# First batch, column 3: ordinary products for all score groups, and the sums of v made one column later

## The chip, the cores and the metric

The kernel runs on one core of one Trainium2 chip. The metric is the device time of one execution in microseconds (us): less is better. The times below are those of six executions, and one further execution was recorded by the hardware profiler. The engines are named as in the profile: PE (TensorE; PEld is its weight load), DVE (VectorE), ACT (ScalarE), POOL (GpSimd) and SP (SyncE). The last two issue most of the transfers here.

## The reference

There are 8 batches of 3008 rows. With S = 3008:

```
scores = (1/S) * z @ z.T                 # per batch, z: 3008 x 64
out    = (relu(scores) ** 2) @ v         # v: 3008 x 256
x      = u * out                         # u: 3008 x 256
h      = x @ w_in                        # 256 -> 2048
y      = (h * cos(h)) @ w_out            # 2048 -> 256
```

The square of the scores is symmetric, because the scores are z times its own transpose.

## The kernel before

**Tiling.** The 3008 rows of a batch are cut into 6 column blocks of 512 (the last has 448). A score group (b, c, R) is the 512x512 piece of the squared scores of batch b between column block c and row block R. It lives in one of 18 SBUF slots, `s0` to `s17`; the trace numbers them from s_70. For each column c the kernel sums, over all six row blocks R, the product of v with the group. The sum stands in two PSUM banks, `acc`, one for each half of the 256 columns of v. `finish` (line 377) multiplies it by u into `x`, and `h_quantum` and `y_quantum` (lines 515, 532) do the two matmuls after that, on tiles of 512 rows.

**Where a group comes from.** By symmetry a group with R > c, once computed, serves column R too, if it is transposed: `turn_s` (line 317) issues a DMA transpose on SP from the slot of the group to a second slot, the turned group. In the first batch the columns 0 to 2 don't wait for that: `direct` (line 234) says that all six of their groups are computed. From column 3 on the groups with R < c come turned. For column 3 of the first batch these are (0,0,3), (0,1,3) and (0,2,3). The list `TURNS` says when the transposes of the first three columns are issued.

**Two ways to multiply.** `av_bank` (line 359) is the ordinary one: for each block of 128 rows and each half of v, one matmul of 512 columns. Four blocks and two halves make 8 of them for one group. `product` (line 459) is the other: a 2x2 scheme with 7 instead of 8 products, of which each takes 2 matmuls of 256 columns for a group, 14 in all. It needs sums: of the group (`a_sums1` and `a_sums2`, lines 440 and 447, on DVE, in place and in an extra slot called "x"), of v (`v_sums`, line 405, three DVE instructions for one row block, kept for the whole batch), and of partial results (`keep`, line 491: three ACT copies and three DVE additions in a column). `seven` (line 254) lists the row blocks of a column that take this way: `WSET`, and none where `direct` holds. So in the first batch column 3 is the first column to use it, for R = 0, 1 and 2.

**Order.** All pieces are put in a list of events with a time and a rank (`at`, line 555), sorted, and issued in that order. The times are in steps, 8 steps to a column; a step comes to about 3 us of the chip. Within each engine that is the order of the instructions, apart from small moves by the layer that records them[...]. Matmuls are chained in one order (`chain`, line 109), and each load that POOL issues is held until the matmul that was issued last before it (`hold`, line 116). Scores are computed in visits (`s_visit`, line 324): up to three halves of groups, each with two matmuls into PSUM (line 270), two relus on ACT (line 306) and one squaring on DVE into the slot (line 308). Six PSUM banks, called `w`, serve scores, h and y alike, and there are three buffers `rt` for the relus and three `c` for the cosines.

**Slots.** `place` (line 590) goes through all lives of groups, turned groups and "x" slots by their first step, and gives each the slot that has been free the longest. A slot whose last reader is a transpose that has not yet landed makes its next writer wait on the chip, whatever the planner thought. At column 3 of the first batch the planner has:

- slot s_80: the group (0,1,3), read by its transpose; next, the "x" slot of column 3
- slot s_84: the group (0,1,4), read by its transpose; next, the group (0,3,4)
- the turned groups (0,0,3), (0,1,3), (0,2,3) in s_75, s_82, s_70

SP's queue has, in this order: (0,0,3), (0,0,4), a transpose of u, (0,0,5), (0,1,3), (0,1,4), (0,1,5), (0,2,3), (0,2,4), (0,2,5), (0,3,4), (0,3,5), and a transpose of u for column 3.

Of the kernel before, what the change touches and what calls it, by code (L numbers as in the profile page):

```python
# [14 lines left out]
def kernel(  # L15
# [25 lines left out]
    NC = NJ // K  # L41
# [5 lines left out]
    U = 8  # L47
# [25 lines left out]
    TSUM = [-2.9, -0.9, -0.8, 3.5, 3.5]  # L73
    XEND = 4.0
    WSET = {0: [0, 1, 2], 1: [0, 1, 2], 2: [0, 1, 2], 3: [0, 1, 2], 4: [0, 1, 2, 3], 5: [0, 1, 2, 3]}
# [28 lines left out]
    def after(ins, other, cls):  # L104
        tc.add_manual_dep(
            ins, other.name,
            mybir.DependencyInfo(cls, mybir.DependencyReason.DATA), reason="order")
# [126 lines left out]
    def direct(b, c, R):  # L234


        return b == 0 and c <= 2
# [15 lines left out]

    def seven(b, c):

        return [] if direct(b, c, c) else WSET[c]

    def s_matmuls(b, c, R, p):

# [75 lines left out]
    def av_half(b, c):  # L335

        a = fresh[(b, c, NC - 1)][K - 1]
        for nh in range(NDH):
            h = slice(nh * JLAST, (nh + 1) * JLAST)
            chain(nc.tensor.matmul(  # L340
                accs[(b, c)][nh],
                vs(b, NG - 1)[h, G - 1, nh * P:(nh + 1) * P],
                a[h], start=False, stop=False, skip_group_check=True))
# [25 lines left out]
    def av_chunk(b, c, blocks, start, last):  # L369
        if start:  # L370
            open_acc(b, c)
        for nh in range(NDH):
            av_bank(b, c, nh, blocks, start, last)
        if last:
            finish(b, c)
# [29 lines left out]
    def v_sums(b, R):  # L405

        j = R * K
        t = vs(b, j // G)[:, j % G:j % G + K, :].rearrange("p (h k) d -> p h k d", h=2)
        o = vsum[R]
        b12, b22 = t[:, :, :, P:2 * P], t[:, 1, :, P:2 * P]  # L410
        left = t[:, 0, :, :].rearrange("p k (d w) -> p d k w", w=P)
        after(nc.vector.tensor_tensor(o[:, 0:3:2], b12, left, ALU.subtract).ins,
              before[-1], NOSYNC)
        nc.vector.tensor_tensor(o[:, 1], b22, o[:, 0], ALU.subtract)
        nc.vector.tensor_tensor(o[:, 3], t[:, 1, :, 0:P], o[:, 1], ALU.subtract)
# [24 lines left out]
    def a_sums1(b, c, R):  # L440
        s1 = quarters(b, c, R, (0, 1))
        after(nc.vector.tensor_tensor(s1, s1, quarters(b, c, R, (1, 1)), ALU.add).ins,
              before[-1], NOSYNC)
        nc.vector.tensor_tensor(  # L444
            second(b, c, R), s1, quarters(b, c, R, (0, 0)), ALU.subtract)

    def a_sums2(b, c, R):

        src = quarters(b, c, R, (1, 0), (0, 1))
        dst = (quarters(b, c, R, (0, 1), (1, -1)) if by_key(b, c, R)  # L450
               else quarters(b, c, R, (1, 0), (-1, 1)))
        h = wide(b, c) // 2
        sub = second(b, c, R).unsqueeze(1).broadcast_to([P, 2, 2, h])
        after(nc.vector.tensor_tensor(dst, src, sub, ALU.subtract).ins,  # L454
              before[-1], NOSYNC)
# [35 lines left out]
    def keep(b, c, n):  # L491
        h = wide(b, c) // 2
        if n == 1:
            parts_of[(b, c)] = (spool.tile([P, 2, CW // 2], FP32, name="p15"),
                                spool.tile([P, 2, CW // 2], FP32, name="q"))
        p15, q = parts_of[(b, c)]
        acc = accs[(b, c)]
        if n in (1, 5):
            nc.scalar.copy(p15[:, n // 5, 0:h], acc[n // 5][:, h:2 * h])
        elif n == 6:  # L500
            nc.vector.tensor_tensor(  # L501
                q[:, 0, 0:h], acc[0][:, h:2 * h], p15[:, 1, 0:h], ALU.add)
        elif n == 8:
            nc.vector.tensor_tensor(
                acc[0][:, 0:h], acc[0][:, 0:h], p15[:, 0, 0:h], ALU.add)
        elif n == 7:
            nc.scalar.copy(q[:, 1, 0:h], acc[0][:, h:2 * h])
        else:
            a = acc[1][:, 0:2 * h].rearrange("p (t h) -> p t h", t=2)
            nc.vector.tensor_tensor(a, a, q[:, :, 0:h], ALU.add)  # L510
# [44 lines left out]
    def at(t, rank, f):  # L555
        events.append((t, rank, len(events), f))
# [5 lines left out]
    span = NC * U  # L562
# [5 lines left out]
    for b in range(B):  # L568
# [6 lines left out]
        for c in range(NC):  # L575
            if direct(b, c, c):
                for i in range(NC):
                    R = (c + i) % NC
# [7 lines left out]
    def use(key, first, last):  # L586
        a, z = lives.get(key, (first, last))
        lives[key] = (min(a, first), max(z, last))
# [16 lines left out]
                use(("a", b, c, R), t, t + 3)  # L605
    for b in range(B):
        for R in range(NW):
            at(b * span + (TSUM[R] if b else 2 * U + R), 2, lambda b=b, R=R: v_sums(b, R))
        for c in range(NC):
            t = b * span + c * U  # L610
            W = seven(b, c)
            d = direct(b, c, c)
            ready = 1.5 + when[(b, c, NC - 1)]
            first, last = (0.6, 6.93) if d else (HALF[c] if W else 1.0, 7.3)
            room = [i for i, sc in enumerate(scores)
                    if max(ready, t + first) < sc[0] < t + last and i not in also]
            if room:
                also[min(room, key=lambda i: scores[i][0])] = lambda b=b, c=c: av_half(b, c)
            else:
                at(t + last, 3, lambda b=b, c=c: av_half(b, c))  # L620
            if d:
                order = [(c + i) % NC for i in range(NC)]
            else:
                order = [R for R in range(NC) if R not in W]
            blocks = [R * K + k for R in order for k in range(K) if R * K + k < NJ - 1]
            if d:
                places = [(t + q + (0.5 if q < U - 1 else -0.05), 3) for q in range(U)]
            elif W:
                for i, R in enumerate(W):
                    at(t + SUM1[c][0] + SUM1[c][1] * i, 2, lambda b=b, c=c, R=R: a_sums1(b, c, R))  # L630
                    use(("x", b, c), t + SUM1[c][0], t + XEND)
                    use(("t", b, R, c) if R < c else ("a", b, c, R), t, t + 6.5)
                    at(t + SUM2[c][0] + SUM2[c][1] * i, 2.5, lambda b=b, c=c, R=R: a_sums2(b, c, R))
                at(t + WADD[c], 2.6, lambda b=b, c=c: keep(b, c, 0))
                at(t + RADD[c], 2.6, lambda b=b, c=c: keep(b, c, 8))
                done = [0, 0]
                for o, what in PLAN[c]:
                    for piece in what.split():
                        if piece[0] == "P":
                            n = int(piece[1])  # L640
                            at(t + o, 2, lambda b=b, c=c, n=n: product(b, c, n))
                            if n in (1, 5, 6, 7):
                                at(t + o + 0.02, 2.1, lambda b=b, c=c, n=n: keep(b, c, n))
                            continue
                        nh, size = "AB".index(piece[0]), int(piece[1:])
                        part = blocks[done[nh]:done[nh] + size]
                        done[nh] += size
                        end = done[nh] >= len(blocks)
                        at(t + o, 2, lambda b=b, c=c, nh=nh, part=part, end=end:
                           av_bank(b, c, nh, part, False, end))  # L650
                        for j in part:
                            R = j // K
                            use(("a", b, c, R) if R >= c else ("t", b, R, c), t + o, t + o + 0.3)
                assert done == [len(blocks)] * 2, (done, len(blocks))
                at(t + 7.45, 2, lambda b=b, c=c: finish(b, c))
                places = []
            else:
                places = [(t + q // 2 * 2 + (1.4 if q % 2 else 1.0), (4, 2)[q % 2])
                          for q in range(U)]
            n = 0  # L660
            for o, size in places:
                part = blocks[n:n + size]
                if part:
                    first, end = n == 0 and not W, n + size >= len(blocks)
                    at(o, 2, lambda b=b, c=c, part=part, first=first, end=end:
                       av_chunk(b, c, part, first, end))
                    for j in part:
                        R = j // K
                        use(("a", b, c, R) if R >= c or d else ("t", b, R, c), o, o + 0.3)
                n += size  # L670
            use(("a", b, c, NC - 1), t, t + last)
# [3 lines left out]
    for m in range(NT):  # L675
        b, i = divmod((m + 1) * TW - 1, S)
# [85 lines left out]
```

## Time and profile before

| What | us |
|---|---|
| median of 6 executions | 1223.8 |
| lowest and highest of them | 1222.83 and 1230.57 |
| the profiled execution, its own time | 1232.27 |
| span of the profiled execution | 1230.1 |
| PE busy in the span | 1207.7 (98%) |
| DVE busy | 1028.4 (84%) |
| ACT busy | 833.4 (68%) |

Rows of the trace give a start and a length in us, and in square brackets the idle time of the engine ahead of the row and what ended it. The view of stages gives, for a stretch of time, the busy time of each engine with the number of its instructions, the granted share of the TensorE clock and the transfers' share and rate. In the view of waits, the numbers are the total, how often, and the longest.

### The profile page before, as it was taken

What the parts mean: (1) busy time and instruction counts of PE and PEld (TensorE: products, weight loads), DVE (VectorE), ACT (ScalarE), POOL (GpSimd) and SP (SyncE); (2) the same over time, 40 slices, a digit from 0 to 9 for tenths busy, and PEclk for the clock granted to TensorE, in tenths of its full rate; (3) what the DMA queues carried; (4) which work ended last, traced back from release to release, by engine and by line L of the source; (5) the groups of instructions that cost most, each with busy time, mean ns of one, the idle gap of its engine ahead of it and who ended that gap; (6) DMA issues with size and microseconds to landing.
All of it is one profiled execution on the core that took longest, in us unless ns stands there. A gap on an engine that the chain in (4) does not pass through costs nothing.

```text
span 1230.1 us, 23076 instructions
## 1 busy us (share of the span) xinstructions
PE 1207.7 (98%) x8439; PEld 769.1 (63%) x8439; DVE 1028.4 (84%) x2073; ACT 833.4 (68%) x1744; POOL 145.9 (12%) x201
## 2 busy tenths in 40 slices
PE   8869999999999999999999999999999999999998
PEld 3336666666666666666666666666666666666666
DVE  8677988889888898888988889888898888888775
ACT  6546767667766677667766677676776767777645
POOL 3201101101011010200101001010010100100000
PEclk9979999999999999999999999999999999999999
DMA  9997987689687786967868779576895757956311
GB/s 143 125 167 119 139 119 125 105 122 135 117 122 120 125 128 118 112 122 118 138 108 123 124 119 142 99 123 118 121 145 108 122 105 114 155 99 118 73 27 51
DMA packets 484225, 145.02 MB, mean 118 GB/s; under 512 B 432400, under 2 KB 484112, under 8 KB 484112
## 3 DMA queue, kind: packets, MB, share of 16 engines
q1 hardware_dynamic: 356448, 88.73, 44.7%
q0 software_dynamic: 100400, 29.77, 24.8%
q10 hardware_dynamic: 27264, 25.06, 6.2%
q8 instruction: 66, 1.08, 0.4%
q14 instruction: 47, 0.39, 0.1%
HBM read 60.29 MB, written 24.64 MB: 69 GB/s over the span
## 4 chain that ended last, share of the span: by engine, by line
PE 95%; DVE 2%; DMA 1%; ACT 1%; SPq 0%; issue 0%; ACTq 0%; DVEq 0%
PE w L536 27%; PE w L519 26%; PE acc L485 19%; PE acc L363 17%; PE w L270 6%; DMA s<-s 1%; PE acc L340 1%; DVE s L308 1%; SPq L320 0%; DVE g L526 0%; PE w L719 0%; ACT rt L306 0%; DVE rt L304 0%; ACT zT L226 0%; DVE s L454 0%
## 5 line engine op out<-in xcount | busy, mean ns | idle before, releaser
L523 ACT ACTIVATE c<-w 128x512 f16<-128x512 f32 x752 | 437.8, 620 | 274.4 <-PE w L519 205.8
L526 DVE TENSOR_TENSOR g<-w,c 128x512 f16<-128x512 f32 x752 | 493.0, 684 | 61.2 <-ACT c L523 58.4
L536 PE MATMUL w<-w_out,g 128*128 128x256 f16 x3008 | 448.6, 273 | 0.0
L519 PE MATMUL w<-x,w_in 128*128 128x512 f16 x1504 | 447.1, 380 | 0.0
L536 PEld LDWEIGHTS <-g 128*128 128x128 f16 x3008 | 294.3, 98 | 191.1
L363 PE MATMUL acc<-s,v 128*128 128x512 f16 (+1 forms) x1000 | 285.9, 378 | 0.1
L306 ACT ACTIVATE rt<-w 128x512 f16<-128x512 f32 x489 | 253.3, 615 | 43.3 <-PE w L270 43.3
L308 DVE TENSOR_TENSOR s<-rt 128x1024 f16<-128x1024 f16 x254 | 172.7, 688 | 88.2 <-ACT rt L306 83.8
L519 PEld LDWEIGHTS <-w_in 128*128 128x128 f16 x1504 | 147.3, 98 | 76.0 <-issue 6.7
L485 PE MATMUL acc<-s,vsum 128*128 128x256 f16 (+1 forms) x1208 | 157.9, 270 | 0.4 <-DVE q L501 0.2
L121 POOL DMA_DIRECT2D ust<-in_u_dram x112 | 81.2, 731 | 565.4 <-PE acc L363 547.3
L363 PEld LDWEIGHTS <-v 128*128 128x128 f16 x1000 | 92.9, 98 | 73.7 <-issue 29.1
L485 PEld LDWEIGHTS <-vsum 128*128 128x128 f16 x1208 | 117.2, 98 | 19.5 <-issue 3.9
L485 PE MATMUL acc<-s,v 128*128 128x256 f16 (+1 forms) x906 | 117.6, 270 | 0.0
L270 PE MATMUL w<-zT 64*128 64x512 f16 (+3 forms) x684 | 92.2, 360 | 17.6 <-DVE g L526 15.5
L485 PEld LDWEIGHTS <-v 128*128 128x128 f16 x906 | 85.4, 98 | 20.4 <-issue 12.4
L454 DVE TENSOR_TENSOR s<-s,s 128x1024 f16<-128x1024 f16 (+1 forms) x151 | 94.8, 670 | 2.7 <-PE acc L485 2.7
L543 ACT ACTIVATE ob<-w 128x256 f32<-128x256 f32 x188 | 71.2, 379 | 10.6 <-PE w L536 10.6
L444 DVE TENSOR_TENSOR s<-s 128x512 f16<-128x512 f16 (+1 forms) x151 | 61.4, 412 | 12.5 <-DMA s<-s 10.6
L287 ACT ACTIVATE rt<-w 128x512 f16<-128x512 f32 (+3 forms) x176 | 62.8, 451 | 10.5 <-PE w L270 10.5
L392 DVE TENSOR_TENSOR x<-acc,ut 128x64 f16<-128x64 f32 (+7 forms) x178 | 68.7, 430 | 0.1
L270 PEld LDWEIGHTS <-zT 64*128 64x128 f16 x684 | 25.6, 94 | 67.6 <-issue 53.9
(37 smaller groups left out, 370.4 us busy)
## 6 DMA issues: line engine op xcount, KB each, us to landing
out_dram<-ob ACTq DMA_DIRECT2D x92, 256.0 KB, 2.3
ust<-in_u_dram POOLq DMA_DIRECT2D x80, 128.0 KB, 4.6
v<-in_v_dram POOLq DMA_DIRECT2D x16, 512.0 KB, 6.5
s<-s SPq DMA_TRANSPOSE x249, 4.4
v<-in_v_dram POOLq DMA_DIRECT2D x8, 448.0 KB, 9.4
zst<-in_z_dram POOLq DMA_DIRECT2D x14, 128.0 KB, 5.1
ust<-in_u_dram POOLq DMA_DIRECT2D x16, 96.0 KB, 4.9
w_in<-in_moe_w_in_dram POOLq DMA_DIRECT2D x4, 256.0 KB, 14.8
```

Of the source, the lines that this page charges most:

```text
L121: hold(nc.gpsimd.dma_start(dst, src))
L270: chain(nc.tensor.matmul(sp[:, s0 * P:], zt[h, R * K + k + 1 - lo, :], zt[h, j0 + s0:j0 + K, :].rearrange("p j w -> p (j w)"), start=True, ...
L306: nc.scalar.activation(rt[:, i, :], banks[k], AF.Relu)
L308: ins = nc.vector.tensor_tensor(t.rearrange("p s k w -> p k s w")[:, 2 * p:2 * p + 2], rv, rv, ALU.mult).ins
L363: chain(nc.tensor.matmul(acc[:, 0:wn], vs(b, j // G)[:, j % G, nh * P:(nh + 1) * P], a, start=(start and n == 0), stop=(last and n == len( ...
L454: after(nc.vector.tensor_tensor(dst, src, sub, ALU.subtract).ins, before[-1], NOSYNC)
L485: chain(nc.tensor.matmul(acc[bank][:, cols], lhs[:, k, :], rhs[:, k, :] if old else rhs[:, :, k * P:(k + 1) * P], start=(n in (1, 5) and i ...
L519: chain(nc.tensor.matmul(hp, w_in16[:, k, ft * P:(ft + 1) * P], x[:, k, :], start=(k == 0), stop=(k == NDH - 1)))
L523: nc.scalar.activation(c16, hp, AF.Sin, bias=math.pi / 2.0, scale=inv_s2)
L526: nc.vector.tensor_tensor(gs[(m, ft // FG)][:, ft % FG, :], hp, c16, ALU.mult)
L536: chain(nc.tensor.matmul(ys[m][:, 0:D], gs[(m, f4)][:, ft % FG, ts * P:(ts + 1) * P], w_out16[:, ft, :], start=(ft == 0), stop=(ft == NFT ...
L543: nc.scalar.activation(obs[m][:, i, :], ys[m][:, 0:D], AF.Copy, bias=0.0, scale=inv_s2)
```

## The change

Column 3 of the first batch takes all its six groups by ordinary products, in eight chunks of four and two row blocks, at 1.0, 1.4, 3.0, 3.4, 5.0, 5.4, 7.0 and 7.4 steps into the column (the `else` branch at line 657). Its "x" slot, its sums of groups and its `keep` steps are then not made. The sums of v of the first batch, first used by column 4 now, are made at steps 25, 26.5, 28 and 29.5 instead of 16, 17, 18 and 19.

```diff
     def seven(b, c):
 
-        return [] if direct(b, c, c) else WSET[c]
+        return [] if (b, c) <= (0, NC // 2) else WSET[c]
...
     for b in range(B):
         for R in range(NW):
-            at(b * span + (TSUM[R] if b else 2 * U + R), 2, lambda b=b, R=R: v_sums(b, R))
+            at(b * span + (TSUM[R] if b else 3 * U + 1 + 1.5 * R), 2, lambda b=b, R=R: v_sums(b, R))
```

The planner then gives slot s_80, after the group (0,1,3), to the group (0,3,3), s_85 to (0,3,4) and s_86 to (0,3,5). The turned groups of column 3 keep their slots. Later lives are spread over other slots than before. SP's queue has the same transposes in the same order as above, and POOL's list of loads is the same.

## The prediction

> **What bounds the kernel now.** The page's first part gives PE 98% of the span, so I looked for where PE stands still. The stages show one hole, in the stretch that the change touches:
>
> ```profile
> 52.00:56.00 4.00, 4.00 (x21) 1.81 (x20) 1.22 (x3) 3.59 (x8) 1.55 (x2) 1.00 1.53 149
> 56.00:60.00 4.00, 1.75 (x9) 0.57 (x8) 0.00 (x0) 0.00 (x0) 0.74 (x1) 1.00 1.66 138
> 60.00:64.00 4.00, 0.00 (x0) 0.00 (x0) 0.15 (x1) 0.00 (x0) 0.00 (x0) 0.52 1.60 170
> 68.00:72.00 4.00, 1.49 (x3) 0.30 (x3) 2.82 (x5) 1.48 (x4) 0.00 (x0) 0.50 1.24 251
> 76.00:80.00 4.00, 4.00 (x25) 2.51 (x24) 3.11 (x7) 2.32 (x6) 0.74 (x1) 0.85 1.09 199
> ```
>
> After the stretch come busy PE (first number), PEld, DVE, ACT, POOL, the granted clock, and the transfers. From about 58 to 74 us nothing but transfers runs, and the clock falls to half. From 90 us on PE is busy in every slice. Next, the waits:
>
> ```profile
> PE w L270 <- DVE g L526: 15.5, 5, 12.7
> DVE s L444 <- DMA s<-s: 10.6, 1, 10.6
> DVE s L308 <- DMA s<-s: 3.6, 1, 3.6
> DVE s L442 <- DMA s<-s: 1.3, 1, 1.3
> ```
>
> PE waits for DVE, and DVE for transposes: three times, and in no other row of that view. The rows in order of time say for which:
>
> ```profile
> 52.54 0.68 DVE L308 TENSOR_TENSOR s<-rt 128x1024 f16<-128x1024 f16 x1
> 57.36 0.39 PE L270 MATMUL w<-zT 64*128 64x512 f16 x2
> 63.84 0.42 DVE L444 TENSOR_TENSOR s<-s 128x512 f16<-128x512 f16 x1 [10.62 <-DMA s<-s]
> 68.80 0.69 DVE L308 TENSOR_TENSOR s<-rt 128x1024 f16<-128x1024 f16 x1 [3.59 <-DMA s<-s]
> 70.48 1.78 PE L270 MATMUL w<-zT 64*128 64x512 f16 x3 [12.73 <-DVE g L526]
> 72.92 0.42 DVE L442 TENSOR_TENSOR s<-s 128x512 f16<-128x512 f16 x1 [1.30 <-DMA s<-s]
> 74.00 0.58 PE L270 MATMUL w<-zT 64*128 64x512 f16 x1 [1.75 <-DVE g L526]
> 74.52 1.89 PE L519 MATMUL w<-x,w_in 128*128 128x512 f16 x4
> ```
>
> At 63.84 the first sum of column 3 writes the "x" slot s_80, which the transpose of (0,1,3) reads: that lands there. At 68.80 the score group (0,3,4) writes s_84: (0,1,4) lands. At 72.92 the sum for R = 2 reads the turned (0,2,3). DVE does its work in order, so the cosine products (line 526) that empty the PSUM banks stand behind all three, and PE behind them.
>
> **What the change does, part by part.**
>
> *Removed wait one, and a new one in its place.* The sums are gone, but s_80 now goes to the group (0,3,3), whose squaring (line 308) stands at the same point of DVE's list, behind the same transpose of (0,1,3). So DVE is still held to about 63.8. Behind it are two more squarings, then the cosine products, for which PE waits. This part of the stall gains nothing. The transfers ahead of it may shift: the sums of v, 12 instructions on DVE at 41 to 49 us, are gone there, but PE is busy without a hole from 36 to 49.6, so PE gets ahead by at most the 1.5 us that it waits for DVE at 50 to 52, and the two loads held behind that point start that much sooner. I take 0, with 0 to 1.5 us of loss.
>
> *Removed waits two and three.* s_84 has no new writer here, and no sum reads the turned (0,2,3). The groups (0,3,4) and (0,3,5) go to s_85 and s_86, which no transpose reads. From 63.84 DVE's list runs: three squarings at 0.68 (65.9), three cosine products at 0.62 (67.7), one u product at 0.64 (68.4), the fourth cosine product (69.0). PE's next h matmul needs that one's bank, so it starts at 69.05 instead of 74.52: 5.5 us earlier. ACT then has five relus at 0.6 to do first (to 70.8), where before it had done most, so the first cosine is 4.8 us earlier. DVE finishes the four cosine products of that round at about 74.7 instead of 80.66, by its own list. Between 4.8 and 6 I take 5.5.
>
> *PE's work.* The chain of waits has both widths back to back:
>
> ```profile
> 28.98 2.69 PE acc L363 x12
> 102.28 2.62 PE acc L485 x24
> ```
>
> That is 0.224 us for 512 columns and 0.109 for 256. Removed: 3 groups x 14 = 42 of the narrow, 4.6 us. Added: 3 x 8 = 24 of the wide, 5.4 us. PE, which bounds the rest of the column, gets 0.8 us more.
>
> *DVE's and ACT's work.* By shape, between 40 and 105 us:
>
> ```profile
> L454 DVE TENSOR_TENSOR s<-s,s 128x1024 f16<-128x1024 f16 x5 | 3.2, 686 | 0.3 <-PE acc L485 0.3
> L444 DVE TENSOR_TENSOR s<-s 128x512 f16<-128x512 f16 x7 | 2.8, 418 | 10.6 <-DMA s<-s 10.6
> L412 DVE TENSOR_TENSOR vsum<-v 128x512 f16<-128x512 f16 x4 | 1.6, 414 | 0.0
> L415 DVE TENSOR_TENSOR vsum<-v,vsum 128x256 f16<-128x256 f16 x4 | 1.1, 278 | 0.0
> ```
>
> Removed from DVE: six sums at 0.42 (lines 442, 444; 2.5 us, inside the hole), three at 0.65 (line 454; 2.0) and three `keep` additions (0.41 + 0.69 + 0.42 = 1.5). The sums of v are 4 x 0.41 + 8 x 0.28 = 3.9 us. Before, the hole paid for them; now they lie at 71 to 90 us, where DVE is nearly full (15 of 16 us from 76 to 92). But the 3.5 us of line 454 and `keep` lay in the same stretch, so DVE gets 0.4 us more there, beside PE. Were DVE the bound it would cost that 0.4. ACT loses three copies at 0.37, hidden. PE's small waits at 80 to 86 us (0.36 + 0.25 in the stages), most of them on those `keep` and sum steps, should go: 0.6 us gained.
>
> *The clock.* The Trainium skill, "TensorE: Matmul & The Clock Gate", Part 1, has the gate look at windows of about 3.4 us: half rate after one idle window, full after a busy one. That speaks against counting the shorter hole as a smaller clock loss: the hole is still 10 us, and the gate still falls. The rows agree: 0.52 in 60 to 64, and 0.85 in 76 to 80, which is half clock to about 77.2, 2.7 us after PE started again. If only the rows' 2.7 us count, before and after lose alike: 0. By the window rule the release steps in 3.4 us from 77.2, so at 70.4 or 73.8: 1.3 or 4.7 us of half-rate work after 69.05, against 2.7; half of the difference is a gain of 0.7 or a loss of 1.0. I take -0.2.
>
> *Transfers.* PE will be 5.5 us earlier, and with it the last load of w_out (issued at 77.56 before, at 71 to 72 now), which then meets the transposes. The same skill, "DMA: Bandwidth & Descriptors", "Queues, rings and completion order", says that each engine takes turns between queues. The rows agree: (0,1,4) landed 5.0 us after (0,1,3) with loads under way, and two transposes followed in 4.1 us. Ordinary products need the turned (0,2,3) only after 30 wide matmuls and the cosines between: at 75.5 to 77 us. Landing at 72.9, or 74 to 75 with its last microsecond or two shared, it is in time. Its cover is 1 to 4 us; beyond it PE waits one for one. The later ones, (0,2,4) and (0,3,4), have some 8 us.
>
> *Sum*: 5.5 - 0.8 + 0.6 - 0.2 = 5.1 us. Against the profiled execution: 1232.3 to 1227.2, its span 1230.1 to 1225.0. The median lies 8.5 us under that execution, and nothing shown says where; if it is in the slow transposes, both kernels' holes move together, since the gain is the distance from the landing of (0,1,3) to that of (0,2,3). So 1223.8 - 5.1 = 1218.7. Own range 1217 to 1220.5.
>
> **Rivals.**
>
> *The hole is as long as before* (15%). The squaring into s_80 leads the visit now, and if (0,1,3) lands 3 to 5 us later, behind loads that come sooner, the gain is spent. For: DVE hangs on this transfer alone. Against: the loads shift by 1.5 us at most. 1222 to 1224.
>
> *More is gained* (15%). In executions whose transposes are quicker than in the profiled one, (0,1,3) lands before PE runs dry, at 57 us; then the new hole is under a window, the clock doesn't fall, and the landings up to (0,2,3), up to 9 us, are all saved. 1214 to 1216.
>
> *Slower* (10%). The late transpose meets PE itself: the first product of R = 2 stands in PE's queue behind a wait for (0,2,3), where DVE's sum had stood. It costs 1 us for each that the landing is after 77. It uses up the gain at 82, and passes no-change by 0.3% from 86 on; with the earlier w_out load and the loads of u in turn, at the 5 us a transpose of the loaded rows, three transposes from 63.8 end at 79, so it takes slower still. 1229.
>
> *The change doesn't do what it says*: not likely, the removed work is in no list of the changed kernel.
>
> **How the numbers follow.** The forecast has 60%. 0.3% is 3.7 us, about what a measurement of this kernel can tell from no change: faster is under 1220.1, slower over 1227.5. Faster: 57 of the 60, and 15 of more gain, 0.72. Same: 3 and 15, 0.18. Slower: 0.10. The range leaves out the slower case and the best few in a hundred: 1214 to 1224.5.
>
> **What would show it.** A hole of PE from about 57 to 69 instead of to 74; before it one long DVE wait at line 308 for a transpose, and no wait at 442 or 444 there; line 363 matmuls in column 3 with no wait for s<-s; h matmuls from 69 us; half clock to 70 to 74. Wrong if PE waits for DMA s<-s at line 363, if the DVE wait ends later than 65, or if later batches, whose slots are shuffled, show DVE waiting for transposes, which before they never do.

## The result, and the profile after

The changed kernel takes 1219.6 us (median of 30 executions, 1213.5 to 1225.8), the kernel before 1226.9 (median of 65 on the same chips, 1219.9 to 1231.8). The ratio is 0.994, with a 95% interval of 0.9926 to 0.9953: 7.3 us less, or 5.8 to 9.1. The forecast had been 5.1 us less. The times of one kernel spread over some 12 us, so each profile below is one execution of that spread. The profiled executions are 1232.3 before and 1225.8 after, with spans of 1230.1 and 1223.7.

The stages of the changed kernel, with columns as before:

```profile
52.00:56.00 4.00, 4.00 (x21) 1.76 (x18) 0.00 (x0) 2.54 (x6) 2.29 (x3) 1.00 1.78 158
56.00:60.00 4.00, 0.66 (x4) 0.11 (x3) 0.00 (x0) 0.00 (x0) 0.00 (x0) 0.88 1.54 161
60.00:64.00 4.00, 0.00 (x0) 0.00 (x0) 1.68 (x3) 0.00 (x0) 0.00 (x0) 0.50 1.50 162
64.00:68.00 4.00, 2.51 (x6) 0.66 (x6) 4.00 (x8) 3.09 (x7) 0.00 (x0) 0.50 1.31 238
72.00:76.00 4.00, 4.00 (x19) 1.70 (x18) 1.32 (x4) 1.13 (x3) 0.00 (x0) 0.91 0.89 121
```

The hole of PE is still there, from 56.7 to 64.9 us, and the clock is at half until about 72.7. The waits of the changed kernel:

```profile
DVE s L308 <- DMA s<-s: 11.5, 1, 11.5
PE w L270 <- DVE g L526: 8.4, 2, 8.2
PE w L519 <- DVE g L526: 0.6, 1, 0.6
```

Three waits of DVE for transposes have become one, at line 308. PE's waits for the cosine products are 9.0 us instead of 15.5. In order of time:

```profile
56.27 0.39 PE L270 MATMUL w<-zT 64*128 64x512 f16 x2
62.32 1.90 DVE L308 TENSOR_TENSOR s<-rt 128x1024 f16<-128x1024 f16 x3 [11.46 <-DMA s<-s]
64.13 1.88 DVE L526 TENSOR_TENSOR g<-w,c 128x512 f16<-128x512 f32 x3
64.87 1.80 PE L270 MATMUL w<-zT 64*128 64x512 f16 x4 [8.21 <-DVE g L526]
67.26 3.57 PE L519 MATMUL w<-x,w_in 128*128 128x512 f16 x8 [0.59 <-DVE g L526]
70.62 3.78 PE L363 MATMUL acc<-s,v 128*128 128x512 f16 x12
75.97 1.89 PE L363 MATMUL acc<-s,v 128*128 128x512 f16 x8
```

The squaring of (0,3,3) into s_80 stands where the first sum stood and waits for the same transpose, which lands at 62.3 here (63.8 before). After it DVE runs through to the cosine products, and PE's h matmuls start at 67.26 instead of 74.52.

Where the gain is made can be read by numbering the 752 cosines of the run (line 523) and taking the start of each from both traces:

| cosine | before, us | after, us | ahead by |
|---|---|---|---|
| 4 (before the hole) | 54.0 | 52.9 | 1.1 |
| 8 (first after it) | 75.6 | 68.3 | 7.3 |
| 28 (column 4) | 105.4 | 99.0 | 6.3 |
| 100 | 218.5 | 212.1 | 6.3 |
| 751 (the last) | 1219.6 | 1213.2 | 6.3 |

All of it is there at 105 us. In the 1100 us after that the lead stays between 6.1 and 6.3 us, though later groups sit in other slots.

### The profile page after: what moved, and what is told of

Read it like the earlier page. It is cut to its first block, busy times and chain, and to the rows that moved or that the text cites. A ratio compares the mean times of both kernels' runs of the same rounds, so it can differ in the third digit from the quotient of the medians.

```text
span 1223.7 us, 23026 instructions
## 1 busy us (share of the span) xinstructions
PE 1208.1 (99%) x8421; PEld 767.5 (63%) x8421; DVE 1024.1 (84%) x2061; ACT 831.9 (68%) x1741; POOL 145.9 (12%) x201
## 4 chain that ended last, share of the span: by engine, by line
PE 97%; DMA 2%; DVE 1%; issue 0%; ACT 0%; DVEq 0%; ACTq 0%
PE w L536 27%; PE w L519 26%; PE acc L485 18%; PE acc L363 18%; PE w L270 6%; DMA s<-s 1%; PE acc L340 1%; DMA v<-in_v_dram 1%; DVE s L308 0%; DVE g L526 0%; ACT rt L306 0%; PE w L719 0%; DVE x L392 0%; PE w L221 0%; ACT ob L543 0%
## 5 line engine op out<-in xcount | busy, mean ns | idle before, releaser
L363 PE MATMUL acc<-s,v 128*128 128x512 f16 (+1 forms) x1024 | 291.6, 379 | 0.3 <-DMA v<-in_v_dram 0.3
L485 PE MATMUL acc<-s,vsum 128*128 128x256 f16 (+1 forms) x1184 | 154.7, 270 | 0.0
L485 PE MATMUL acc<-s,v 128*128 128x256 f16 (+1 forms) x888 | 115.1, 270 | 0.0
L121 POOL DMA_DIRECT2D v<-in_v_dram x40 | 31.2, 786 | 297.1 <-PE acc L485 144.1
```

The costliest lines, as they stand in the source:

```text
L121: hold(nc.gpsimd.dma_start(dst, src))
L363: chain(nc.tensor.matmul(acc[:, 0:wn], vs(b, j // G)[:, j % G, nh * P:(nh + 1) * P], a, start=(start and n == 0), stop=(last and n == len( ...
L485: chain(nc.tensor.matmul(acc[bank][:, cols], lhs[:, k, :], rhs[:, k, :] if old else rhs[:, :, k * P:(k + 1) * P], start=(n in (1, 5) and i ...
```

## The experiments

Besides the time of a kernel I give, from its trace, when the transpose of (0,1,3) landed and how long PE waited, at 50 to 100 us, for DVE's cosine products or for a transpose. Where no instruction waited for the landing, it is the last completion count of that transfer in the trace.

| run | median us | ratio (95%) | span profiled | (0,1,3) lands | PE's wait |
|---|---|---|---|---|---|
| before | 1226.9 | 1 | 1230.1 | 63.8 | 15.5 |
| changed | 1219.6 | 0.994 (0.9926 to 0.9953) | 1223.7 | 62.3 | 9.0 |
| sums of v back | 1217.1 | 0.9947 (0.9924 to 0.9971) | 1212.3 | 51.8 | 1.0 |
| slots | 1220.6 | 0.9946 (0.9921 to 0.9971) | 1220.4 | 59.1 | 6.6 |
| order | 1220.9 | 0.9927 (0.9905 to 0.9949) | 1221.0 | 60.0 | 5.1 |
| slots and order | 1214.1 | 0.9906 (0.987 to 0.9941) | 1214.0 | 50.8 | 0.7 |
| z late | 1215.2 | 0.9915 (0.9884 to 0.9945) | 1213.1 | 51.8 | 0.9 |
| before, z late | 1223.4 | 0.9977 (0.9956 to 0.9998) | 1218.6 | 51.0 | 4.5 |
| before, slots | 1226.4 | 1.0007 (0.9987 to 1.0027) | 1223.9 | 55.1 | 9.1 |
| w_out early | 1224.8 | 0.998 (0.9956 to 1.0005) | 1225.2 | 64.6 | 11.4 |
| w_out early, slots and order | 1215.6 | 0.9914 (0.9878 to 0.9949) | 1212.4 | 57.9 | 0.2 |
| column 3 ordinary in all batches | 1223.3 | 0.9988 (0.9967 to 1.0009) | 1221.5 | 56.0 | 3.3 |
| all of them (see below) | 1215.6 | 0.9916 (0.9892 to 0.994) | 1212.4 | 50.2 | 1.0 |

Each ratio is to the kernel before, timed beside that run. Its median there was 1226.9, 1226.7, 1224.6 or 1228.2 us, depending on the run, so runs are best compared by their ratios. In these thirteen traces, one of each kernel, the same transpose lands at anything from 50 to 65 us, and the profile that the prediction was argued from is at the late end.

### The sums of v at their old place

```diff
-            at(b * span + (TSUM[R] if b else 3 * U + 1 + 1.5 * R), 2, lambda b=b, R=R: v_sums(b, R))
+            at(b * span + (TSUM[R] if b else 2 * U + R), 2, lambda b=b, R=R: v_sums(b, R))
```

> The changed kernel, with the sums of v of the first batch made at steps 16 to 19 again, so that column 3's ordinary products are all that is left of the change. My theory: the sums of v (3.9 us of DVE) lie again in the time for which DVE waits for the transpose of (0,1,3) anyway, and after the hole DVE has 3.9 us less to do; PE bounds there, so the time stays that of the changed kernel, within 1 us (0.6% under the kernel before). The rival, that moving the sums of v brought a part of the gain, expects 1.5 to 4 us more than the changed kernel. The opposite rival, that the move costs, expects 1 to 4 us less.

The ratio is 0.9947 against 0.994: no difference within their intervals of about 0.2%. So the move of the sums of v is worth nothing that these runs can tell, and the other half of the change, ordinary products in column 3, is the whole of it. The interval still allows up to about 3 us either way, so a cost under that is not excluded.

This run's profile happened to catch an early landing, and shows the changed column 3 without a hole. Its stages:

```profile
52.00:56.00 4.00, 4.00 (x21) 1.79 (x20) 3.42 (x7) 3.62 (x8) 2.14 (x3) 1.00 1.73 197
56.00:60.00 4.00, 3.75 (x19) 1.29 (x18) 3.33 (x7) 2.80 (x6) 0.14 (x1) 1.00 1.52 221
60.00:64.00 4.00, 4.00 (x21) 1.82 (x19) 3.67 (x6) 3.15 (x7) 0.74 (x1) 1.00 1.03 172
```

PE is full but for 0.25 us, the clock does not fall, and the span is 1212.3 us. The 30 times of the changed kernel fall into 14 at 1213.5 to 1216.0 and 16 at 1218.7 to 1225.8. The mean granted clock, which is on record for each execution, divides them in nearly the same way: it is 1.0 in 13 of the 14 and 0.998 in the other, and 0.994 to 0.999 in all of the 16. So about half of its executions have no hole that costs clock. The kernel before had a clock of 1.0 in one of the 128 executions that were timed beside the experiments.

### Slots for the squarings, and the order of the products

Three runs: slots chosen by hand, own row blocks first, and both.

```diff
+    PICK = {('a',0,3,3): 15, ('a',0,3,4): 16, ('a',0,3,5): 8, ('a',0,4,4): 9, ...}
...
-            f = min(fit) if fit else min(free)
+            own = [f for f in fit if f[1] == PICK.get(key)]
+            f = own[0] if own else min(fit) if fit else min(free)
...
                 order = [R for R in range(NC) if R not in W]
+                if not W:
+                    order = order[c:] + order[:c]
```

> The changed kernel, with slots chosen by hand so that no squaring near column 3 writes a slot which a transpose under way reads: (0,3,3), (0,3,4), (0,3,5) and (0,4,4) get the slots of groups that were never turned. My theory: DVE's wait of 11.5 us at line 308 goes, PE runs on from 56 us, and meets the late transposes itself: about 1 us at the first product of (0,1,3), to its landing at 62, and some 5 us at the first product of (0,2,3), to its landing at 70. Column 3's first product of (0,2,3) then starts at about 70.5 instead of 76.4: 5 to 6 us under the changed kernel, a ratio of about 0.989 to the kernel before. The rival, that the order of the transfers sets the end of the stretch whatever waits for them, expects no gain over the changed kernel (ratio 0.994).

> The changed kernel, with own row blocks first in column 3, and the planner's own slots. My theory: DVE is still held at the squaring of (0,3,3) into s_80 until (0,1,3) lands, and with it PE, so the order alone gives nothing where there is a hole: the times are those of the changed kernel, near 1215 and near 1223, a ratio of 0.992 to 0.996 to the kernel before. The rival, that the order of the products is what frees PE, expects all times at 1214 to 1216, a ratio under 0.991.

> As the run with chosen slots, and column 3 takes its own row blocks 3, 4, 5 first and the turned ones 0, 1, 2 last. My theory: the turned (0,2,3) is then needed only some 6 us later, PE has no hole longer than 2 us between 50 and 90 us, and the clock is not halved there: 9 to 11 us under the changed kernel, a ratio of 0.985 to 0.987 to the kernel before. The rival, that something else than the transposes (DVE's or ACT's work, up to 4 us each) fills the hole as soon as it is closed, expects at most 7 us under the changed kernel.

*Slots alone* give 0.9946, as the rival had it, and not 0.989. The wait at line 308 is gone, but the trace shows what took its place:

```profile
63.80 0.59 PE L363 MATMUL acc<-s,v 128*128 128x512 f16 x2
70.82 2.72 PE L363 MATMUL acc<-s,v 128*128 128x512 f16 x6 [6.43 <-DMA s<-s]
```

PE itself waits 6.4 us at the first product of the turned (0,2,3). The theory had that wait at 5 us and the product at 70.5; it came at 70.8, where the changed kernel had it at 76.4. What it left out is that the clock falls for this hole too: it is half from 69.3 to 76.1, so 5.3 us of work after the hole ran at half rate. Of the 5.6 us won at that point 3.3 are left in the span (1220.4 against 1223.7), and in executions with an early landing there was nothing to win.

*Order alone* is at the changed kernel's time, as expected. Its waits at line 308 (7.6 us) and of PE (5.1) are of the same kind.

*Both together* give 0.9906, from four executions, all at 1213.9 to 1216.3. Its profile is of an early landing (50.8), so it shows that nothing else fills the hole, but not what becomes of a late one. The expected 9 to 11 us against the changed kernel were 5.5 by the medians, and some 4 by the ratios: they were reckoned against an execution with a hole, and half of the changed kernel's have none.

### Loads beside the transposes: z later, w_out earlier

```diff
-            at(t - 3.5 * U, 0, lambda b=b: load_z(b))
-            at(t - 2.5 * U, 0, lambda b=b: turn_z(b))
+            at(t - (3.5 if b > 1 else 2.75) * U, 0, lambda b=b: load_z(b))
+            at(t - (2.5 if b > 1 else 2.25) * U, 0, lambda b=b: turn_z(b))
```

```diff
-                at(17 + 2.5 * q, 0, lambda q=q: load_w_out(q))
+                at(11 + 1.5 * q, 0, lambda q=q: load_w_out(q))
```

> The changed kernel, with the five loads of z of the second batch at step 26 instead of 20, and their transposes at step 30 instead of 28. It leaves the slots as they are and takes away transfers that run beside the transposes of (0,0,5) and (0,1,3). My theory: these loads take turns with the transposes on the transfer engines, so (0,1,3) lands 3 to 6 us earlier (56 to 59 us), DVE's wait at line 308 is shorter by as much, the hole is under 5 us, and the time is 3 to 6 us under the changed kernel. The rival, that SP's queue or the transposes' own sources set when they land, expects the landing at 62 and no gain.

> The changed kernel, with the four loads of w_out at steps 11, 12.5, 14 and 15.5 instead of 17, 19.5, 22 and 24.5. It doubles the suspected cause: 1 MB of loads then runs beside the first transposes. My theory: (0,1,3) lands 3 to 8 us later than without, every execution has the hole of PE, and the time is 1222 to 1229, a ratio of 0.998 to 1.003 to the kernel before. The rival, that the landings spread for a reason that the loads have no part in, expects the changed kernel's two groups of times again, near 1215 and near 1223.

> The run with chosen slots and own row blocks first, with the loads of w_out as early as in the run before this one. My theory: late transposes cost it little, since nothing before the last third of column 3 needs them: 1214 to 1219, at least 5 us under the changed kernel with early w_out. The rival, that late transposes hold up column 3 in any order, expects less than 3 us between the two.

With z late, all five executions lie at 1214.5 to 1217.6, (0,1,3) lands at 51.8 in the profile, where 56 to 59 were expected, and PE's wait is 0.9 us. The time is 4.4 us under the changed kernel by the medians and some 3 by the ratios; 3 to 6 were expected. With w_out early, all 12 lie at 1221.2 to 1228.4, so the group near 1215 is gone, as expected. The waits of that run:

```profile
DVE s L308 <- DMA s<-s: 13.9, 1, 13.9
PE w L270 <- DVE g L526: 10.8, 2, 10.6
```

The landing at 64.6 is 2.4 us later than in the changed kernel's profile, where 3 to 8 were expected. Loads moved away from the transposes leave no execution in the late group (of five), and loads moved on to them leave none in the early one (of twelve), so where the loads stand decides how often the landing is late. The transfers of the kernel before show the sharing: in the 6 us from 56 its transposes moved 0.57 MB beside 0.30 MB of loads, and in the 3 us from 68, alone, 0.79 MB.

Why one execution of a kernel is early and the next late is not shown by this. The loads of z are issued from 46 to 48 us on, depending on the trace. In the eight traces in which they and w_out stand at their old places, the transpose of (0,0,4), two places before (0,1,3) among those of groups, lands at 39.9 to 47.2 us, and (0,1,3) follows nearly in the same order, at 50.8 to 63.8. So much of the difference is there before these loads begin. And with z late the kernel before still spreads over 11 us (below).

The third run tells what the late landing costs when nothing early needs it. With w_out early, slots and order it takes 1215.6, which is 9.1 us under the same loads without them. Its (0,1,3) lands at 57.9 in the profile, later than the 56.0 at which another run's DVE still waited 5.1 us, and PE's wait is 0.2 us. Two of its five executions are at 1220.2 and 1221.2; their granted clock is 0.998 and 0.997, where the other three have 1.0, 1.0 and 0.998. No trace of such a one was taken, and why they are longer is open.

### All of them

All edits above but the early w_out, on the changed kernel.

> Chosen slots, own row blocks first, the loads of z of the second batch later, and the sums of v at steps 16 to 19 again, all on the changed kernel. My theory: no execution of it has a hole of PE between 50 and 90 us, so all its times lie together at the time of the executions without a hole, 1213.5 to 1216.5, a ratio of 0.989 to 0.991 to the kernel before. The rival, that the spread of times has another cause than the landing of the transposes, expects times up to 1220 and more among them, as with the changed kernel.

0.9916, median 1215.6. Seven of ten executions are at 1214.3 to 1216.9, three at 1218.9 to 1221.7, so the expectation that none would be above 1216.5 failed. The profile (span 1212.4) has no hole. The three have a granted clock of 0.997 to 0.999, and six of the seven others have 1.0, so they too lost some clock. No trace of one was taken. They may have this hole after all, or lose the clock elsewhere: in the trace of the run with the order alone it is half from 11.3 to 14.7 us as well, long before column 3. So the rival, another cause of the spread, is not excluded.

### The kernel before, with each part of its wait taken away

The first run gives its "x" slot, (0,3,3) and (0,3,4) other slots (the same code as above, with three entries); the second moves the loads of z.

> The kernel before, with the x slot of column 3 and the group (0,3,3) moved to slots of groups that were never turned, and (0,3,4) to the slot of (0,1,3), which the sum for R = 1 waits for anyway. It takes away the two waits in which a slot is rewritten, and leaves the sums that read the turned (0,1,3) and (0,2,3). My theory: the sum for R = 2 still holds DVE to the landing of (0,2,3), and with it the cosine products and PE, so nothing is gained: a ratio of 0.998 to 1.002 to the kernel before. The rival, that the change's gain came from the rewritten slots, expects 4 to 7 us less (0.994 to 0.997).

> The kernel before, with the loads of z of the second batch at step 26 and their transposes at step 30, as in the run of the changed kernel with late z. My theory: the transposes of (0,1,3) and (0,1,4) land before DVE gets to them, and (0,2,3) at about 64 us, so of the three waits the third alone is left; PE's hole is 6 to 9 us, and all times lie at 1220 to 1224, which is 6 to 8 us above the changed kernel with late z. The rival, that early landings take the hole away here too, so that the change is worth only what the late landings make of it, expects 1214 to 1217.

New slots alone: 1.0007, no gain, as expected. Its waits are all at the sums that read turned groups:

```profile
DVE s L442 <- DMA s<-s: 8.5, 2, 7.0
PE w L270 <- DVE g L526: 9.1, 6, 7.7
```

The longer one ends at 65.33, the landing of (0,2,3). So of the three waits of the kernel before, the last one alone keeps the hole, and the change could gain only because it does not have that sum.

Late z in the kernel before: 1223.4, a gain of 0.2% with an interval that nearly touches none. The profile has (0,1,3) landing at 51.0, (0,2,3) at 60.5, and of the three waits the third alone, as expected:

```profile
DVE s L442 <- DMA s<-s: 3.4, 1, 3.4
```

Its hole is 3.5 us where 6 to 9 were expected, and half clock lasts 6.8. The range of times was wider than expected, 1216.1 to 1227.5, with four of 20 under 1217.1 and at a clock of 0.999 or 1.0, so in some executions the third wait too seems to cost no hole. With z late in both, the changed kernel (1215.2) is 8.2 us under this one by the medians, and 7.6 by the ratios, where 6 to 8 were expected.

### The price of ordinary products, seven times

```diff
-        return [] if (b, c) <= (0, NC // 2) else WSET[c]
+        return [] if (b, c) <= (0, NC // 2) or c == NC // 2 else WSET[c]
```

> The changed kernel, with column 3 by ordinary products in all eight batches instead of the first alone. It measures the disputed price of the ordinary products seven times, where no transfer is waited for. My theory: 0.8 us of PE for each column, as reckoned from the widths (24 x 0.224 against 42 x 0.109), and PE bounds there, so seven more columns cost 5 to 6 us: 1224 to 1226, a ratio of 0.998 to 0.999 to the kernel before. The rival, that 6 us less of DVE in each such column is worth as much as PE loses, expects the changed kernel's time (ratio 0.994) or less.

0.9988, as expected. The trace has it without the spread: by the starts of the cosines it was 13.81 us ahead of the kernel before at cosine 100, and 8.63 at the last. Seven columns cost 5.2 us, 0.74 each. DVE's relief of some 6 us in each of them, the sums and additions that the prediction counts, buys nothing that shows.

## Why the prediction was right, and what it mis-sized

**The new wait in place of the first** is as predicted: one wait at line 308 for the transpose of (0,1,3), no gain in it, and in this execution loads sooner by 1.1 us without a later landing.

**The second and third waits**: predicted start of the h matmuls 5.2 us after the landing (69.05 after 63.84), measured 4.9 (67.26 after 62.32). Of the 7.3 us by which they came earlier, 1.5 are the earlier landing of that one execution, 5.7 the change: predicted 5.5. The run with new slots in the kernel before shows that the third wait did the holding. The prediction's sentence that nothing but transfers runs from 58 to 74 us was too strong: by its own rows DVE is busy for 2.8 and PE for 1.5 of the 4 us from 68.

**PE's work**: 0.8 predicted, 0.74 measured as the mean of seven columns. The 0.6 us of small waits at 80 to 86 us came as predicted: PE is full in all stages of the changed kernel from 68 to 88 us.

**The sums of v**: 0.4 us at most predicted, none seen within 3 us.

**The clock**: predicted to come back at 70.4 or 73.8, measured 72.7. The two instants were steps of 3.4 us counted from the profile before, but where the steps lie is different in each execution: half clock starts at 60.12 before and at 59.04 after. 5.4 us of work from the h matmuls on ran at half clock instead of 2.7, which by my estimate costs 1.35 (half of the difference), where the sum had 0.2. So the profiled executions differ by 6.3 us, of which 1.5 are the landing: 4.8 for the change where there is a hole, against 5.1 predicted. The terms as measured add up to 4.2, so 0.6 is not accounted for.

**Transfers**: the product of (0,2,3) was predicted for 75.5 to 77 and came at 76.4; its transpose had landed at 70.6, in time.

**The term that was mis-sized** is the last one, how the profiled execution stands to the median. The prediction said that both kernels' holes move together with the landings, so that the gain stays. It does not. When (0,1,3) lands before PE runs dry, the changed kernel has no hole and no clock loss at all, while the kernel before mostly still waits for (0,2,3). That is argued from the traces of the two kernels with z late, and from the clock of 1.0 in 13 executions of the one and in one of 128 of the other. The prediction had it as a rival, "more is gained", at 15%, with 1214 to 1216; 14 of 30 executions are of that kind, and they pull the median from 1222.4, that of the other 16, to 1219.6. The 8.5 us between the profiled execution and the median of before were the sign: the profile was a late one (1232.3, above each of the 65), and I took it as typical.

That rival's reason does not hold as it stood, that a hole under 3.4 us keeps the clock. The run with column 3 ordinary in all batches has no wait of PE over 1.8 us, 3.3 in all, and loses clock:

```profile
56.00:60.00 4.00, 1.74 (x9) 0.44 (x7) 3.87 (x7) 1.28 (x3) 0.00 (x0) 1.00 1.47 204
60.00:64.00 4.00, 3.20 (x10) 1.12 (x9) 4.00 (x8) 3.52 (x8) 0.00 (x0) 0.57 1.38 236
```

**Luck**: the forecast time, 1218.7, is nearer to the measured 1219.6 than the forecast change is to the measured one: 5.1 us lies outside the interval of 5.8 to 9.1. It was counted from a median of six executions, 1223.8, where 65 gave 1226.9. A start that was 3.1 too low and a change that was 2.2 too small nearly cancel.

## What to carry to other kernels

When a wait is removed, look at what stands next in that engine's queue and what its buffer was used for last: here the same transfer held the next writer of the slot, and a choice of slots alone only moved the wait to PE. A wait on a transfer that shares the transfer engines with loads has no fixed length; when the profiled execution is well above the median, ask whether the wait in it is the usual one, and reckon the change with the transfer early as well as late. Consumers of late transfers belong last, and loads that can wait belong behind the transposes: with w_out early, chosen slots and own row blocks first were worth 9 us. On the changed kernel as it is, they, the late loads, and both together came out 3 to 5 us lower, with intervals that overlap its own.

## What the runs showed of the hardware

I had not expected that the same transpose lands at anything from 50 to 65 us, nor that the stretches of half clock come in steps: 3.41, 6.83, 10.24, 13.65 and 17.07 us in these traces, all multiples of 3.413. (A last one, around the end of the work, is cut short by the end of the record.)

The prediction's window rule, half rate after one idle window, is too strict for these traces: with the steps counted back and on from where such a stretch begins, PE need not stand still for a whole step. The clock fell after steps of which PE was busy 30% (55.6 to 59.0 us of the changed kernel), 33% (57.1 to 60.5 of the run with column 3 ordinary in all batches) and 46% (56.5 to 59.9 of the kernel before with late z), and did not after one of 56% (62.5 to 65.9 of the run with chosen slots). It stayed at half through a step of 82% (65.9 to 69.3 of the changed kernel) and came back after one of 83% (60.5 to 63.9 of the run in all batches). I read no threshold from this: the run with the order alone lost the clock after a step of 67% (7.9 to 11.3 us).
